# Splitting the first quad's k load by key blocks, and a new order, in a fused attention and feed-forward kernel

## The chip, the cores and the metric

One Trainium2 chip, one of its cores. The metric is the device time of one execution in microseconds (us). A core has TensorE (PE in the profile; PEld are its weight loads), VectorE (DVE), ScalarE (ACT), GpSimd (POOL) and SyncE (SP), each with its own instruction stream that is worked off in order, and 16 DMA engines that all the queues share. "SPq" and "POOLq" are DMA issues of SP and POOL.

## The reference

```python
batch, n_heads, seq, head_dim = 8, 12, 448, 64          # q, k, v: float32
scores = matmul(q, k.transpose(0, 1, 3, 2)) / sqrt(64)
attn = maximum(scores, 0.0) ** 2 / 448
x = matmul(attn, v)                                      # then [B, S, H*D] -> [3584, 768]
h = x @ w_in                                             # [768, 2048]
g = h * (1 / (1 + exp(-1.702 * h)))
out = g @ w_out                                          # [2048, 768], float32
```

## The kernel before

**Units of work.** A batch has 12 heads; four heads make a quad, so there are 24 quads, u = 0 to 23. A quad's q, k or v lies in a tile of 128 partitions x 2 x 448: a partition stands for one of two heads and one of 64 runs of 7 tokens, the middle axis for the other pair of heads, and the 448 columns are those 7 tokens of 64 numbers each. Block j is the j-th token of every run. Matmuls run in float16.

**Attention of one quad.** k and q come as float32 by a load on SP's queue (`load`, L97) and are cast on an engine (`cast`, L107), or, for quads 1 to 5, are cast on the way by a load on POOL's queue (`load_cast`, L102), which v always is. They are turned around: quads 0 to 5 by 14 transposes on TensorE against an identity (`trans_pe`, L126) and a copy out of PSUM (`trans_evac`, L136), later ones by a DMA transpose on SP's queue. `scores` (L143) makes four 64 x 64 x 448 matmuls for one block j of keys, into two PSUM banks; `relu` (L156, on ACT or DVE) copies each bank out, `square` squares both halves, `attn_v` (L173) sums over the seven blocks, and `xt_evac` copies the result to x.

**Feed-forward.** Tokens go in eight groups g of 6 or 8 blocks of 64. Group 0's first layer is 16 column parts f of six full matmuls (`m1`, in three steps); the other groups take a seven-product scheme on sums of blocks (`unit_product`), so do all groups in the second layer (`pair_product`, `single`). A gelu on ACT writes a float32 buffer (`gf`, five of them), a widening on POOL or DVE turns it into the float16 tile that the second layer reads.

**The order.** No scheduler decides it at run time: a string of some 1950 words is worked off from left to right, and each word emits one step on its engine, so every engine's stream is in the order of the words. A word is a letter for the step, its indices, `:` and an engine where that differs from the usual one, `@` and the PSUM banks (0 to 7) that it takes. `s4.0@5.4` is the scores of quad 4, block 0, in banks 5 and 4; `r4.2.1` the relu of quad 4, block 2, bank 1 of its two; `x` a square; `a3` the attention product of quad 3; `tk`, `ek` the transposes and the copy out of k (`tq`, `eq` of q); `f0.6.1` a step of the first layer; `g` a gelu, `v` a widening (usual engine POOL); `Lk`, `Lq` loads on SP; `jk`, `jq`, `V`, `jwa`, `jwb`, `jo` loads of k, q, v, w_in (two halves of each of four blocks) and w_out on POOL; `K`, `Q` casts; `G3` a small transfer on SP that waits for w_in's block 3 and so holds back the loads behind it; `I` the identity, on POOL; `z13` thirteen matmuls on zeros that write a bank nobody reads.

**The loads on POOL's queue** are 28 before the first widening stands in that stream: the float16 k, q, v of the first quads, w_in, and last the four of w_out. They use eight semaphores in turn, so the n-th load waits for the landing of the one eight before it. A transfer into a reused buffer also waits for that buffer's last reader.

**The opening of the string before**, up to the first scores, is

```python
"jq1 jk1 V0 z13@0 Lk0 K0:d z1 I tk0@1 Lq0 Q0:d jk3 ek0:a tq0@2 tq1@3 jq3 eq0 eq1 "
"s0.1@4.5 r0.1.1 r0.1.0:d s0.4@6.7 r0.4.1:d jq2 s0.6@0.1 r0.6.0:d r0.4.0 V1 r0.6.1 "
```

and around the attention product of quad 3

```python
"f0.6.0@3 f0.6.1 r4.3.0 r4.2.0:d r4.1.1 f0.6.2 g0.6 tk5@7 tq5@0 x3.6 r4.3.1:d eq5:a "
"x4.2 s4.0@5.4 v0.6 s4.4@1.2 ek5 r4.0.1 a3@3.6 r4.0.0:d S2.1 S0.3 v0.2 s4.5@0.7 "
```

Of the kernel before, what the change touches and what calls it, by code (L numbers as in the profile page):

```python
# [8 lines left out]
F32 = mybir.dt.float32  # L9
# [6 lines left out]
def kernel(  # L16
# [43 lines left out]
    def new(tag, shape, dt, name=None):  # L60
        return pools[tag].tile(shape, dt, name=name or tag, tag=tag)
# [35 lines left out]
    def load(n, u):  # L97
        x = new(f"{n}st", [128, 2, S], F32)
        nc.sync.dma_start(out=x, in_=quad(n, u))
        units[u][n + "st"] = x  # L100
# [25 lines left out]
    def trans_pe(n, p, u):  # L126
        ps = bank(p, "tr", F16)
        x = units[u].pop(n + "16")
        for j in range(J):
            for a in range(2):  # L130
                nc.tensor.matmul(  # L131
                    out=ps[64 * a:64 * a + 64, j * 128:(j + 1) * 128],
                    lhsT=x[:, a, 64 * j:64 * j + 64], rhs=ident[:, :], is_transpose=True)
        units[u][n + "ps"] = ps

    def trans_evac(n, e, u):  # L136
        t = new(f"{n}T", [128, J, 128], F16)
        copy(e, t, units[u].pop(n + "ps")[:, 0:J * 128].rearrange("p (j c) -> p j c", j=J))
        units[u][n + "T"] = t
# [283 lines left out]
    with tc.manual_schedule():  # L423
# [8 lines left out]
        for n in "kq":  # L432
            two["L" + n] = lambda e, p, u, n=n: load(n, u)
            two["j" + n] = lambda e, p, u, n=n: load_cast(n, u)
            two[n.upper()] = lambda e, p, u, n=n: cast(n, e, u)
            two["R" + n] = lambda e, p, u, n=n: trans_dma(n, u)
            two["t" + n] = lambda e, p, u, n=n: trans_pe(n, p, u)
            two["e" + n] = lambda e, p, u, n=n: trans_evac(n, e, u)
# [20 lines left out]
        def zeros(e, p, n):  # L459
# [8 lines left out]
            "jq1 jk1 V0 z13@0 Lk0 K0:d z1 I tk0@1 Lq0 Q0:d jk3 ek0:a tq0@2 tq1@3 jq3 eq0 eq1 "  # L468
            "s0.1@4.5 r0.1.1 r0.1.0:d s0.4@6.7 r0.4.1:d jq2 s0.6@0.1 r0.6.0:d r0.4.0 V1 r0.6.1 "
            "s0.3@2.3 r0.3.1:d tk1@5 ek1:a s0.0@4.7 r0.0.0 x0.1 s1.4@0.6 r1.4.0:d r0.3.0 r1.4.1 "  # L470
            "s0.2@1.3 r0.0.1 r0.2.0:d s0.5@5.4 r0.5.1:d r0.2.1 r0.5.0 s1.1@0.2 jk2 x0.3 x0.2 "
            "s1.0@6.7 r1.0.1 x0.0 tk3@1 r1.1.1 r1.1.0 jwa0 jwb0 x0.5 x1.4 r1.0.0 s1.5@4.3 x0.4 jwb2 "
            "tq3@5 jq4 r1.5.1 s1.2@7.2 s1.6@0.6 r1.5.0 x1.0 x0.6:a eq3 jk4 V2 jwa2 a0@3.4 r1.6.1:d "
            "tk2@5 ek3 r1.6.0 ek2 x1.1:a tq2@6 eq2 r1.2.1 r1.2.0 e0.0.1:a s1.3@1.0 x1.2 x1.6 jwa1 "
            "r1.3.1 jwb1 s2.3@5.6 s2.1@2.7 e0.1.1:a r1.3.0 x1.3 x1.5 r2.3.0 jk5 jq5 r2.1.1:d e0.0.0 "
            "s2.2@0.4 r2.3.1 r2.2.0 r2.2.1 a1@1.5 s3.0@7.6 x2.3:a e1.0.0:a r2.1.0:d V3 s2.0@0.4 "
            "e1.1.0 r2.0.0 e0.1.0 s2.6@2.1 jwb3 r3.0.0:d r3.0.1 s2.4@0.3 r2.6.0:d f0.3.0@7 f0.2.0@6 "
            "r2.6.1 r2.4.1:d r2.0.1 r2.4.0:d s3.2@2.1 s2.5@3.4 e1.0.1:a x2.2 f0.2.1 r3.2.1 r2.5.1 "
            "x2.1 r3.2.0 r2.5.0:d f0.3.1 x2.0:a x2.6:a s3.3@0.1 tq4@4 tk4@2 e1.1.1 V4 x2.4 r3.3.1 "
            "x2.5 jwa3 eq4 r3.3.0 a2@3.5 e2.0.1:a e2.0.0 S0.1 s3.1@1.4 ek4:a x3.3 V5 e2.1.0 jo0.0 "  # L480
            "jo1.0 f0.1.0@0 f0.1.1 f0.2.2 f0.1.2 S0.2 r3.1.1 r3.1.0 x3.1 e2.1.1:a f0.3.2 g0.1 x3.2 "
            "g0.2 f0.0.0@2 f0.0.1 x3.0 f0.0.2 g0.0 f0.8.0@3 g0.3 s3.4@4.1 r3.4.1 s3.5@5.0 r3.5.1 "
            "r3.5.0:d s3.6@6.2 r3.6.1 r3.4.0:d f0.8.1 v0.0:d x3.5 x3.4 f0.8.2 jo1.1 r3.6.0 f0.4.0@7 "
            "f0.4.1 f0.4.2 s4.2@1.0 jo0.1 G3 g0.8 v0.3 g0.4 r4.2.1 s4.1@5.2 r4.1.0 v0.4 s4.3@4.6 "
            "f0.6.0@3 f0.6.1 r4.3.0 r4.2.0:d r4.1.1 f0.6.2 g0.6 tk5@7 tq5@0 x3.6 r4.3.1:d eq5:a "
            "x4.2 s4.0@5.4 v0.6 s4.4@1.2 ek5 r4.0.1 a3@3.6 r4.0.0:d S2.1 S0.3 v0.2 s4.5@0.7 "
            "s5.0@4.5 r4.4.0 e3.0.0 e3.0.1:a f0.5.0@1 f0.5.1 f0.5.2 r5.0.0:d f0.10.0@3 x4.0 f0.10.1 "
            "r4.4.1 x4.4 r5.0.1 r4.5.1 r4.5.0 x4.5 f0.10.2 g0.5 g0.10 v0.10 s5.1@6.4 r5.1.0:d "
            "x4.1:a v0.5 r5.1.1 s4.6@2.5 s5.2@7.0 r5.2.1 r5.2.0 r4.6.1:d f0.9.0@1 x4.3 f0.7.0@3 "
            "f0.7.1 f0.7.2 f0.11.0@6 f0.11.1 f0.11.2 g0.7 r4.6.0:d x4.6:a f0.9.1 f0.9.2 S0.4 g0.11 "  # L490
            "s5.4@4.0 Lk6 g0.9 x5.1 s5.5@7.5 r5.4.1:d a4@3.2 r5.5.0 r5.4.0:d s5.6@6.1 r5.6.1 v0.7 "
            "s5.3@0.7 Lq6 r5.3.0 f0.12.0@4 x5.2 S1.1 S3.1 v0.9:d r5.3.1 r5.6.0 x5.3 f0.12.1 x5.0 "
            "f0.15.0@1 e4.0.0:a f0.14.0@0 f0.15.1 f0.15.2 r5.5.1 S2.2 x5.4 x5.5 f0.13.0@7 f0.13.1 "
            "x5.6:a u1.0.0@6 a5@3.5 Q6:a v0.8 v0.11 T1.1 f0.12.2 e4.0.1:a v0.1:d g0.15 t1.0.0 K6 "
            "S1.2 e5.0.1 u1.1.0@2 t1.1.0 u1.3.0@1 e5.0.0 u1.1.1@5 T1.2 u1.0.2 S2.3 t1.0.2 S1.4 "
            "f0.13.2 u1.0.1@3 T1.3 v0.15 g0.13 u1.0.4 f0.14.1 t1.0.4 S3.2 S1.3 v0.13 b1.0.1 T1.4 "
            "W0.1 u1.1.2 u1.0.3 Lk7 Lq8 u1.2.0@7 g1.0.1 v1.0.1 t1.1.2 u1.1.4 b1.1.1 g1.1.1 W2.1 "
            "u1.1.3 t1.1.4 u1.0.5 S3.3 b1.0.3 u1.0.6 b1.1.3 W1.1 u1.1.6 v1.1.1 g1.0.5 u1.2.1@6 W3.1 "
            "v1.0.5 b1.0.6 u1.3.1@3 g1.1.3 v1.1.3 g1.0.3 t1.2.0 b1.1.6 u1.2.2 W2.2 f0.14.2 g1.1.6 "
            "v1.1.6 W3.3 b1.2.1 g1.0.6 v1.0.6:d S3.4 p0.0.0@5 v1.0.3:d t1.3.0 u1.3.2 g0.12 K7 "  # L500
            "t1.2.2 W0.3 S2.4 g0.14 Q8:a u1.2.3 v0.14 u1.2.4 t1.2.4 W0.2 b1.3.1 v0.12:d Rk6 u1.1.5 "
            "g1.2.1 W1.2 A0.0.1@0 b1.2.3 g1.3.1 u1.3.3 W3.2 u1.2.5 p0.0.1@4 g1.1.5 v1.2.1 A0.0.2@1 "
            "g1.2.5 Rq6 h0.0.0 v1.2.5 l0.0.1 s6.0@0.2 g1.2.3 r6.0.1 r6.0.0 V6 u1.2.6 W0.4 t1.3.2 "
            "s6.1@7.2 r6.1.1 p0.0.2 A0.0.3 r6.1.0 W2.4 V8 x6.0:a h0.0.2 u1.3.4 b1.2.6 s6.5@0.2 "
            "r6.5.0 r6.5.1 Lk8 v1.1.5:d s6.2@7.6 r6.2.0 W2.3 p0.0.3 r6.2.1:d W1.3 v1.2.3 x6.5 Lq7 "
            "s6.3@0.2 t1.3.4 K8:p W3.4 r6.3.0 Rk7 b1.3.3 s6.4@7.6 p0.0.4 x6.2:a W1.4 A0.0.4 r6.4.0 "
            "h0.0.4 u1.3.5 r6.4.1 u1.3.6 l0.0.3 g1.3.5 b1.3.6 Q7 x6.4 r6.3.1 p0.0.5 l0.0.5 Rq7 "
            "s7.2@0.7 r7.2.1:d x6.3:a r7.2.0 s6.6@6.1 r6.6.1 r6.6.0:d s7.0@3.2 r7.0.0 x6.1 x6.6 Rq8 "
            "p0.0.6 r7.0.1 s7.1@5.7 g1.3.6 v1.3.6 l0.0.6 s7.4@0.1 r7.4.1 Rk8 a6@6.3 r7.4.0:d Lk9 "
            "x7.2 s7.3@2.4 s7.5@1.0 r7.1.0 x7.0:a V7 p1.0.0@5 r7.1.1:d K9:p Lq9 r7.5.0 r7.5.1:d "  # L510
            "e6.0.0 x7.4 s7.6@7.1 e6.1.1:a r7.3.0 o0.1 e6.0.1:a s8.2@0.2 r8.2.0:d g1.3.3 i0.2.0@3 "
            "r7.6.1:d e6.1.0 v1.3.1:d v1.3.5 r7.3.1 Q9 Lk11 x7.5:a r7.6.0:d x7.1 Rq9 x7.3:a "
            "s8.1@0.1 r8.2.1 n0.2.0:a s8.0@6.4 r8.1.1 Lq10 Q10 x7.6 r8.1.0 r8.0.0 A0.2.5@0 a7@7.2 "
            "e7.1.0:a r8.0.1:d e7.0.1:a e7.0.0 s8.3@3.1 r8.3.1 A1.0.1@1 r8.3.0 s8.6@0.6 r8.6.0 "
            "K11:d i0.2.1@4 h1.0.0:d s8.4@7.1 r8.6.1:d x8.2:a x8.1:a A1.0.2@0 s8.5@3.0 r8.5.0:d "
            "x8.6:a p1.0.1@6 r8.4.1 e7.1.1:a x8.0 p1.0.2 V13 r8.4.0 r8.5.1 Rk9 s9.3@3.1 n0.2.1:a "
            "s9.0@2.7 x8.3 x8.4 x8.5:a r9.3.1:d r9.0.1 l1.0.1 a8@0.4 r9.0.0:d s9.1@1.7 r9.1.1:d "
            "T2.1 g1.2.6 p1.0.3 e8.1.0:a v1.3.3 e8.0.0:a e8.1.1 Lk10 K10:p u2.1.0@2 r9.3.0 e8.0.1:a "
            "T2.2 T2.4 r9.1.0 t2.1.0 Lq11 s9.4@7.0 r9.4.1:d s9.2@3.4 r9.2.0 v1.2.6:d u2.1.1@1 "
            "b2.1.1 u2.1.2 u2.0.0@0 T2.3 t2.0.0:d u2.0.1@3 r9.4.0 Rq10 r9.2.1 Q11:a Rk10 t2.1.2:d "  # L520
            "b2.0.1 g2.1.1 v2.1.1 g2.0.1 A1.0.3 A1.2.1@1 v2.0.1 u2.2.0@7 u2.2.1@4 t2.2.0 u2.1.4 "
            "t2.1.4 b2.2.1 u2.0.2 u2.1.3 b2.1.3 u2.0.3 u2.2.2 t2.0.2 g2.2.1 g2.1.3 u2.0.4 u2.2.3 "
            "Lk12 u2.1.6 x9.3 t2.0.4 u2.0.5 Rk11 v2.2.1 K12 b2.0.3 b2.1.6 h1.0.2 v2.1.3 Lq12 t2.2.2 "
# [147 lines left out]
```

## Time and profile before

| | |
|---|---|
| median of 3 runs | 363.47 us (363.39, 363.47, 364.65) |
| the profiled execution | 364.18 us |
| its span (first to last recorded work) | 362.4 us |
| POOL, busy | 111.8 us (31%) |
| loads of k, q on POOL's queue, median to landing | 8.4 and 6.9 us |
| loads of v, of a half block of w_in, of a w_out part on it | 5.5, 12.7 and 19.9 us |
| loads of k, q on SP's queue | 4.5 and 4.3 us |
| memory read, written | 45.61 MB, 11.01 MB |

The profile is one execution; times inside it count from the start of its span. In a line of the timeline stand start, duration, engine, source line, operation, output and input tiles, the number of instructions merged into it, and in brackets how long the engine idled before and what ended that. In the view by stretches, each engine's busy time stands with the number of its instructions, then the granted TensorE clock, the share of the DMA engines in use (over 1 where queues overlap) and GB/s. The chain that ended last is followed backward from the last instruction, at each step to what released it. Where one merged line covers many matmuls its time is that of the stream, not of one.

### The profile page before, as it was taken

The page shows a single profiled execution, that of the slowest core. Times are in us where ns is not written, and L with a number is a line of the kernel's source. Part 1 is how long each engine was busy: PE and PEld are TensorE (multiplying, and loading weights), DVE is VectorE, ACT ScalarE, POOL GpSimd, SP SyncE. Part 2 cuts the span into 40 slices and gives each one's busy share as a digit, 9 for nine tenths or more (in the row PEclk, how much of TensorE's full clock was granted, in tenths as well). Part 3 has the DMA queues.
Part 4 walks back from the last instruction along what each step waited for, and adds up shares of the span by engine and source line. Part 5 has one row for each costly group of instructions (what it writes and reads, how often), then busy time and mean ns, then how long its engine had stood idle before and what let it go on. Part 6 is the DMA issues. An engine that isn't in the chain of part 4 may idle for free.

```text
span 362.4 us, 9114 instructions
## 1 busy us (share of the span) xinstructions
PE 352.5 (97%) x3598; PEld 236.0 (65%) x3598; DVE 309.1 (85%) x585; ACT 284.9 (79%) x560; POOL 111.8 (31%) x165
## 2 busy tenths in 40 slices
PE   8789999999999999999999999999999999999995
PEld 4445558855579555886569855786559855678662
DVE  3999999999997999888999799868999789875643
ACT  3999996999989997779996899878897697445420
POOL 5744522354225440155014440165021311001200
PEclk9999999999999999999999999999999999999999
DMA  8999999479999989535893764874590233003124
GB/s 182 173 200 201 215 231 228 107 149 220 196 209 189 241 158 260 165 110 79 203 213 77 216 81 118 147 152 104 115 171 4 47 110 89 2 0 89 44 67 110
DMA packets 65228, 51.39 MB, mean 142 GB/s; under 512 B 35744, under 2 KB 61856, under 8 KB 65184
## 3 DMA queue, kind: packets, MB, share of 16 engines
q1 hardware_dynamic: 48256, 36.32, 42.2%
q0 software_dynamic: 16608, 14.09, 27.0%
q8 instruction: 28, 0.46, 0.6%
q10 hardware_dynamic: 320, 0.39, 0.4%
q14 instruction: 16, 0.13, 0.1%
HBM read 45.61 MB, written 11.01 MB: 156 GB/s over the span
## 4 chain that ended last, share of the span: by engine, by line
PE 90%; DMA 5%; DVE 2%; POOL 1%; issue 0%; ACT 0%
PE hx L203 32%; PE ox L203 31%; PE sc L150 9%; PE av L181 8%; PE os L203 6%; DMA q<-in_q_dram 3%; PE ht L228 3%; DMA k<-in_k_dram 2%; PE zp L463 1%; PE tr L131 1%; DVE at L88 1%; POOL wout L415 0%; DVE at L161 0%; POOL q L104 0%; POOL v L104 0%
## 5 line engine op out<-in xcount | busy, mean ns | idle before, releaser
L163 ACT ACTIVATE at<-sc 128x448 f16<-128x448 f32 x218 | 108.2, 567 | 10.7 <-PE sc L150 9.9
L161 DVE TENSOR_SCALAR at<-sc 128x448 f16<-128x448 f32 x118 | 69.5, 614 | 3.6 <-PE sc L150 3.2
L203 PEld LDWEIGHTS <-win 128*128 128x128 f16 x672 | 61.5, 98 | 8.4 <-issue 1.8
L88 DVE TENSOR_TENSOR at<-at 128x896 f16<-128x896 f16 x109 | 65.9, 633 | 0.9 <-ACT at L163 0.2
L217 POOL TENSOR_SCALAR go<-gf 128x512 f16<-128x512 f32 x42 | 28.2, 671 | 109.9 <-ACT gf L214 108.3
L88 DVE TENSOR_TENSOR gf<-hx,gf 128x512 f32<-128x512 f32 (+1 forms) x84 | 51.6, 627 | 11.0 <-ACT gf L79 7.9
L214 ACT ACTIVATE gf<-gf 128x512 f32<-128x512 f32 (+1 forms) x84 | 47.5, 587 | 13.2 <-DVE gf L88 11.8
L169 ACT ACTIVATE at<-at 128x896 f16<-128x896 f16 x59 | 56.5, 974 | 1.1 <-DVE at L161 0.8
L217 POOL TENSOR_SCALAR ge<-gf 128x384 f16<-128x384 f32 x52 | 29.3, 563 | 73.3 <-ACT gf L214 60.8
L150 PE MATMUL sc<-qT,kT 64*64 64x448 f16 x672 | 48.9, 358 | 2.6 <-DVE qT L83 0.9
L203 PEld LDWEIGHTS <-winS 128*128 128x128 f16 x504 | 46.1, 98 | 5.5 <-issue 0.9
L79 ACT ACTIVATE gf<-hx 128x512 f32<-128x512 f32 (+1 forms) x63 | 34.5, 554 | 18.5 <-PE hx L203 15.0
L203 PE MATMUL ox<-wout,go 128*128 128x384 f16 x256 | 46.3, 326 | 0.0
L203 PEld LDWEIGHTS <-go 128*128 128x128 f16 x320 | 30.1, 98 | 22.0 <-issue 4.3
L203 PE MATMUL hx<-T,winS 128*128 128x256 f16 (+1 forms) x336 | 39.9, 261 | 0.0
L181 PE MATMUL av<-at,v 64*64 64x448 f16 x672 | 36.8, 350 | 0.9 <-ACT gf L214 0.6
L203 PEld LDWEIGHTS <-ge 128*128 128x128 f16 x256 | 24.0, 98 | 18.4 <-issue 4.5
L203 PE MATMUL hx<-xo,win 128*128 128x256 f16 x288 | 35.9, 273 | 0.0
L203 PE MATMUL ox<-wT,asum 128*128 128x384 f16 x192 | 34.9, 327 | 0.0
L150 PEld LDWEIGHTS <-kT 64*64 64x64 f16 x672 | 17.6, 105 | 24.7 <-issue 18.0
L203 PEld LDWEIGHTS <-asum 128*128 128x128 f16 x224 | 21.0, 98 | 15.7 <-issue 2.8
L181 PEld LDWEIGHTS <-v 64*64 64x64 f16 x672 | 20.3, 107 | 13.4 <-issue 2.9
(77 smaller groups left out, 452.2 us busy)
## 6 DMA issues: line engine op xcount, KB each, us to landing
out_dram<-osb SPq DMA_DIRECT2D x52, 192.0 KB, 3.9
kst<-in_k_dram SPq DMA_DIRECT2D x19, 448.0 KB, 4.5
qst<-in_q_dram SPq DMA_DIRECT2D x19, 448.0 KB, 4.3
v<-in_v_dram POOLq DMA_DIRECT2D x24, 224.0 KB, 5.5
win<-in_moe_w_in_dram POOLq DMA_DIRECT2D x8, 384.0 KB, 12.7
wout<-in_moe_w_out_dram POOLq DMA_DIRECT2D x4, 768.0 KB, 19.9
q<-in_q_dram POOLq DMA_DIRECT2D x5, 224.0 KB, 6.9
k<-in_k_dram POOLq DMA_DIRECT2D x5, 224.0 KB, 8.4
```

The source lines that it names most:

```text
L79: nc.scalar.activation(out=o, in_=i, func=AF.Copy)
L88: eng[e].tensor_tensor(out=o, in0=x, in1=y, op=op)
L131: nc.tensor.matmul(out=ps[64 * a:64 * a + 64, j * 128:(j + 1) * 128], lhsT=x[:, a, 64 * j:64 * j + 64], rhs=ident[:, :], is_transpose=True)
L150: nc.tensor.matmul(out=sc[a][c, 0:S], lhsT=st["kT"][r, j, c], rhs=st["qT"][r, :, c], start=True, stop=True)
L161: nc.vector.tensor_scalar(out=o, in0=i, scalar1=0.0, scalar2=None, op0=ALU.max)
L163: nc.scalar.activation(out=o, in_=i, func=AF.Relu)
L169: nc.scalar.activation(out=at, in_=at, func=AF.Square)
L181: nc.tensor.matmul(out=av[s][64 * a:64 * a + 64, 0:S], lhsT=v16[r, a, 64 * j:64 * j + 64], rhs=at[r, a, :], start=(j == 0), stop=(j == J - 1))
L203: nc.tensor.matmul(out=o, lhsT=lhs(i), rhs=rhs(i), start=start and i == 0, stop=i == n - 1, skip_group_check=True)
L214: nc.scalar.activation(out=o, in_=i, func=AF.Gelu_apprx_sigmoid, scale=1.0 / SC)
L217: eng[e].tensor_scalar(out=o, in0=i, scalar1=SC, scalar2=1.0, op0=ALU.mult, op1=ALU.mult)
L228: nc.tensor.matmul(out=hp[g, f][:, 0:n], lhsT=w[:, i, fo:fo + 128], rhs=xts[g][:, i, 0:n], start=i == 0, stop=i == NK - 1)
```

## The change

The load, the cast, the transposes and the copy out can now each do one part of a tile, by an index h: part 0 is key blocks 0 to 3 (256 columns), part 1 blocks 4 to 6 (192 columns). Only k of quad 0 uses it. Its two loads stand behind the load of q on SP's queue; before, the whole k stood ahead of q. The zero products go from 14 in one row to 9, then two single ones behind the transposes of k's first part. The whole string of words is another one: the same steps apart from these, in another order, with other banks, and some relus, squares, copies and casts on other engines.

```diff
+    KH = (slice(0, 256), slice(256, S))
+
+    def load(n, u, h=None):
+        st = units[u]
+        if not h:
+            st[n + "st"] = new(f"{n}st", [128, 2, S], F32)
+        c = slice(0, S) if h is None else KH[h]
+        nc.sync.dma_start(out=st[n + "st"][:, :, c], in_=quad(n, u)[:, :, c])
...
+    def cast(n, e, u, h=None):
+        if h is not None:
+            if h == 0:
+                units[u][n + "16"] = new(f"{n}16", [128, 2, S], F16)
+            x = units[u][n + "st"] if h == 0 else units[u].pop(n + "st")
+            copy(e, units[u][n + "16"][:, :, KH[h]], x[:, :, KH[h]])
+            return
...
+    def trans_pe(n, p, u, h=None):
         ps = bank(p, "tr", F16)
-        x = units[u].pop(n + "16")
-        for j in range(J):
+        x = units[u][n + "16"] if h == 0 else units[u].pop(n + "16")
+        for j in range(J) if h is None else range(4 * h, 4 + 3 * h):
...
+        j = slice(0, J) if h is None else slice(4 * h, 4 + 3 * h)
+        copy(e, st[n + "T"][:, j, :],
+             st.pop(n + "ps")[:, 0:J * 128].rearrange("p (j c) -> p j c", j=J)[:, j, :])
...
-            "jq1 jk1 V0 z13@0 Lk0 K0:d z1 I tk0@1 Lq0 Q0:d jk3 ek0:a tq0@2 tq1@3 jq3 eq0 eq1 "
-            "s0.1@4.5 r0.1.1 r0.1.0:d s0.4@6.7 r0.4.1:d jq2 s0.6@0.1 r0.6.0:d r0.4.0 V1 r0.6.1 "
...
+            "Lq0 Q0:d jk1 I z9@0 tq0@1 eq0:a jq1 Lk0.0 K0.0:d tk0.0@2 V0 ek0.0 z1 z1 s0.0@3.4 "
+            "r0.0.1 Lk0.1 K0.1:d s0.3@5.6 r0.3.1:d r0.0.0 x0.0 tk1@7 r0.3.0 s0.1@1.2 r0.1.0 "
+            "r0.1.1:d jq2 tk0.1@0 s0.2@4.6 ek0.1:a s0.6@3.5 jk3 x0.3 r0.2.1 jk2 tq1@1 r0.2.0 "
...
+            "f0.8.2 s4.3@1.7 r3.5.1 g0.1 x3.5 s4.2@3.5 g0.8 v0.8 r3.4.0 x3.3:a s4.1@2.0 r4.1.1 "
+            "r4.3.1 f0.6.0@4 f0.6.1 f0.6.2 g0.6 f0.4.0@6 S2.1 r4.1.0:d r4.3.0:d f0.4.1 f0.4.2 g0.4 "
+            "v0.4 tk5@0 r4.2.0:d tq5@7 r4.2.1 x4.3 s4.4@4.2 s4.0@1.6 x3.4:a a3@3.5 ek5 eq5 r4.0.1 "
...
```

The loads on POOL's queue go, before, in the order jq1 jk1 V0 jk3 jq3 jq2 V1 jk2 jwa0 jwb0 jwb2 jq4 jk4 V2 jwa2 jwa1 jwb1 jk5 jq5 V3 jwb3 V4 jwa3 V5 and the four of w_out; now jk1 jq1 V0 jq2 jk3 jk2 jq3 jwb0 V1 jwa0 V2 jq4 jk4 jwb2 jwa1 jwa2 jwb1 jq5 jk5 V3 jwa3 jwb3 V5 V4 and the four of w_out.

## The prediction

> **What bounds the kernel now.** I read the page's busy shares first, then the busy time by stretches of time, then the timeline of the opening, then the chain that ended last around the point where TensorE's idling stops.
>
> ```profile
> span 362.4 us, 9114 instructions
> ...
> PE 352.5 (97%) x3598; PEld 236.0 (65%) x3598; DVE 309.1 (85%) x585; ACT 284.9 (79%) x560; POOL 111.8 (31%) x165
> ```
>
> TensorE (PE) is busy for 352.5 of 362.4 us, so 9.9 us is all that any order of the work could take from its idle time. The stretches say where those 9.9 us are.
>
> ```profile
> core 0: us, PE busy (x) PEld busy (x) DVE busy (x) ACT busy (x) POOL busy (x), PEclk, DMA share, GB/s
> 0.00:9.06 9.06, 7.49 (x72) 4.48 (x73) 3.25 (x8) 2.98 (x5) 5.11 (x12) 1.00 0.85 182
> 9.06:18.10 9.04, 7.07 (x106) 3.73 (x105) 9.04 (x18) 9.04 (x19) 6.38 (x10) 1.00 1.17 173
> 18.10:40.00 21.90, 19.82 (x278) 11.36 (x282) 20.85 (x44) 20.66 (x46) 11.53 (x16) 1.00 1.30 200
> 40.00:80.00 40.00, 40.00 (x385) 27.03 (x377) 38.55 (x74) 36.10 (x71) 15.04 (x22) 1.00 0.99 186
> ...
> 340.00:362.40 22.40, 18.12 (x116) 11.02 (x113) 11.39 (x20) 4.65 (x9) 2.17 (x3) 0.99 0.34 90
> ```
>
> From 40 us on TensorE has no idle time at all until its last matmul at 358.1; the 4.3 us after that are the last add and the stores. The idle time is in the first 40 us: 1.57, 1.97 and 2.08 us in the three first stretches. There VectorE (DVE) and ScalarE (ACT) are full from 9 us on and the DMA engines are full too (share over 1). So the end is the moment at which TensorE passes its last wait, plus a sum of matmuls that does not depend on how it got there. That last wait is at 39.30, where a3, the attention product of quad 3, starts:
>
> ```profile
> 24.64 11.21 DMA q<-in_q_dram
> 36.13 0.87 POOL wout L415
> 37.27 0.88 POOL wout L415
> 38.22 0.52 POOL ge L217
> 38.76 0.50 ACT gf L214
> 39.30 1.52 PE av L181 x28
> ```
>
> Read upward: a3 needs a PSUM bank that the gelu g0.6 empties; that gelu is the seventh, there are five gf buffers, DVE's widening v0.0 has freed one for the sixth, and the first widening on GpSimd (POOL) frees the next at 38.74; that widening stands in POOL's queue behind the four issues of w_out, and these wait for earlier loads to land. The last of the four is issued at 37.27 after the load of v for quad 3 (issued 25.34, 11.6 us to landing: 36.94). ACT sits idle 0.82 us before g0.6, TensorE 0.61 us before a3. This is the gate for all that follows.
>
> **The change part by part.** Counted from the two word lists, every matmul of the two kernels is the same but for three zero products; there is one more load issue on SP, one more cast and one more copy out of PSUM. All other differences are order.
>
> *The opening.* These rows price it:
>
> ```profile
> 1.15 4.66 PE L463 MATMUL zp<-wT 128*128 128x384 f16 x14 [1.15 <-DVE wT L456]
> 4.29 0.63 DVE L83 CAST k<-kst 128x896 f16<-128x896 f32 x1 [3.19 <-DMA kst<-in_k_dram]
> 5.48 0.63 DVE L83 CAST q<-qst 128x896 f16<-128x896 f32 x1 [0.56 <-DMA qst<-in_q_dram]
> 5.75 0.96 PE L131 MATMUL tr<-ident,k 128*64 128x128 f16 x14
> 6.75 0.92 ACT L79 ACTIVATE kT<-tr 128x896 f16<-128x896 f16 x1 [4.52 <-PE tr L131]
> 8.02 0.95 PE L150 MATMUL sc<-qT,kT 64*64 64x448 f16 x16 [0.33 <-DVE qT L83]
> 8.45 2.22 DVE L161 TENSOR_SCALAR at<-sc 128x448 f16<-128x448 f32 x4
> ```
>
> Now q goes first on SP's queue and takes k's landing: 4.24, cast until 4.92. Its 14 transposes (0.96) run 4.95 to 5.91, the copy by ACT (0.92) ends at 6.87. The first 256 of 448 columns of k land between q's 4.24 and 5.46, when all of the second load had landed; in proportion 4.24 + 1.22 x 256/448 = 4.94. Cast 0.63 x 4/7 = 0.36 to 5.30 (5.82 at worst), 8 transposes behind q's, 8/14 of 0.96 = 0.55, to 6.46, copy by DVE 4/7 of its 0.58 = 0.33, to 6.8. Then come two zeros of 4.66/14 = 0.333 each, 6.46 to 7.12. So the first score is at about 7.1 instead of 8.02: 0.9 earlier, with bounds 0 (the extra SP issue of 0.45 and the cast push k back to where it was) and 1.15 (zeros free, ACT's copy decides at 6.87). The first relu moves with it, 8.45 to 7.5. The second part of k (cast 0.27, six transposes 0.41, copy 3/7 of 0.92 = 0.39) lies beside the relus of the first blocks. The three zeros that go (3 x 0.333 = 1.0) lie in time in which TensorE waits for q anyway: nothing.
>
> *Rule against it.* 333 ns a zero of 384 columns, against 8 products of 384 columns in 1.30 us (163 ns) later: at the start TensorE runs at half its later pace, though the granted clock reads 1.00, and the first 14 transposes take 0.96 against 0.58 for later ones. The Trainium skill (TensorE: Matmul & The Clock Gate, part 1) says the array runs at half rate until about 3.4 us of sustained activity, and that idling returns it there. Nine zeros end at 1.15 + 3.0 = 4.15, and TensorE then idles until 4.95. By the rule the first scores may run at half pace, some 0.2 us later each; by the rows of before they would not. Either is smaller than the slack found below.
>
> *The load of k for quad 2.* Before, it is the eighth load on POOL's queue, lands at 18.34 and TensorE, DVE and ACT idle 0.86, 0.80 and 0.41 us around it. Now it is sixth; the sixth load of before (q of quad 2, issued 8.4) landed at 15.3, and it is wanted at about 17. That wait goes: worth 0 to 0.8, I take 0.5, since DVE and ACT, not TensorE, set the pace there.
>
> So ACT, DVE and TensorE come to the gate 0.9 + 0.5 = 1.4 us earlier (0 to 2.0), with the same work done: up to it both kernels have 31 scores, 21 first-layer parts, 43 relus on ACT; what moves between ACT and DVE nearly cancels (ACT: one copy and one square more, 0.3 + 1.0, and 0.92 x 3 less 0.92 + 0.39 of k/q copies saved).
>
> *The gate itself.* The new order has the same gate: the sixth gelu, g0.6, takes the buffer that DVE's v0.3 frees, the seventh, g0.4, waits for POOL's first widening, v0.8, and that stands behind the same four w_out issues, the last of them again waiting for v of quad 3, again the 20th load of POOL's queue with the same 19 ahead of it, in another order. The DMA engines are full between (about 200 GB/s), so it lands when those bytes are through. What can move it is the start of that queue: 144 GB/s between 7 and 9 us, when little more than v of quad 0 and a load issued at 7.01 was in flight. Now a load is issued at about 5.95, when q's transposes are done. At 200 instead of 144 these 2 us carry 112 KB more, 0.56 us. Against that, the next loads are issued 0.3 to 0.6 later than before (they wait for transposes of k in two steps). I take 0.5 earlier, bounds 1.2 earlier (the low rates up to 13 us filled as well) and 0.8 later.
>
> *Behind the gate.* Before, a3 followed g0.6 at once. Now g0.4 is followed on ACT by the relu r4.2.1 (0.47), which frees one of a3's two banks, and the square x3.4 (0.97), which a3's fifth block needs: a3 starts 0.5 later and loses some 0.25 inside. Less two switches between half-array and full matmuls that no longer lie behind this point, 0.11 each (ox of 8: 1.41 after scores, 1.30 otherwise). Together +0.5.
>
> *After it.* Before lost nothing there, so a new order can only lose: I add 0.1, bounds 0 and 1.0; The queues that the order moves have cover there. On SP the gate on w_in block 3 now waits for the 22nd load of POOL's queue, not the 21st, so k and q of quad 6 behind it go out some 2 us after the 39.85 and 40.45 of before; their casts by ACT began at 52.5, so 8 us cover it, and beyond that quad 6's first score (73.0) would be late. On POOL v of quad 4 falls from 22nd to 24th place, landing near 42.9 where it was 40.6; a4 starts near 47.3. The w_out parts change places; their first sum by DVE was at 59.5. The end (last product, add, stores) has the same steps.
>
> Sum against the profiled execution, span 362.4: -0.5 + 0.5 + 0.1 = +0.1; the 1.4 us saved in the opening is spent waiting at the gate. The profiled execution took 364.18, 1.8 more than its span and 0.7 above the median of the runs, 363.47 (363.39 to 364.65). Since before and after are read against that median, and the bounds lean to the fast side, I set 363.3.
>
> **The rivals.** (1) The gate opens with the opening: the loads run ahead by 1.2 or more, and the order behind g0.4 costs nothing, so 1.2 to 2.0 of the earlier start reaches the end: 361.5 to 362.3. For it: 7 to 13 us shows 144, 169, 124 GB/s, room to fill. Against: POOL issued the loads that landed in 9 to 18 us four or more us ahead, so issue was not their limit. (2) Slower: POOL's queue falls behind. Loads five to seven wait for transposes in TensorE's own order; if they come 0.8 late and nothing refills it, v of quad 3 lands at 37.7, and with the 0.5 behind the gate and a later stall of up to 1.0 the time is 364.5 to 365.8. It decides from the point where that landing is later than 36.94. For it: the issue times; against: the queue of eight loads is full from 13 us on. (3) The change does not do what it says: k's first part lands with the second, the first score stays at 8.0. The gate hides this: 363.5, the forecast's time.
>
> **How the numbers follow.** Forecast, gate holds (rival 3 within it): 0.56, own range 362.7 to 364.1. Rival 1: 0.27. Rival 2: 0.17. A difference of 0.5% (1.8 us) is about what a measurement of this kernel can tell from no change. Faster by more (under 361.65) is about two thirds of rival 1, 0.18; slower by more (over 365.3) needs most of rival 2's terms at once, 0.10; the rest 0.72. The range takes in both rivals but for their far ends: 361.5 to 365.0.
>
> **What would show it.** First score near 7.1; the idle before the transposes of quad 2's k gone; POOL's first widening again near 38; ACT idle 1.5 to 2.5 us before g0.4; a3 within 0.5 of 39.3; no idle of TensorE later. It is wrong if a3 starts before 38.3 or after 40.3, or if TensorE idles behind it.

## The result, and the profile after

The changed kernel takes 369.21 us (median of 4 runs, 368.82 to 369.55) where the kernel before takes 363.59 beside it: ratio 1.0148, 95% interval 1.0125 to 1.0171. It is slower, by 5.6 us; the forecast was no change (363.3). The profiled execution took 369.55, its span is 5.3 us longer than before. The page's first lines, the changed kernel:

```profile
span 367.7 us, 9122 instructions
...
PE 354.4 (96%) x3595; PEld 236.3 (64%) x3595; DVE 311.7 (85%) x578; ACT 285.4 (78%) x566; POOL 113.9 (31%) x168
```

Busy times hardly move, so the loss is waiting and stretched work. Its busy times by stretches:

```profile
core 0: us, PE busy (x) PEld busy (x) DVE busy (x) ACT busy (x) POOL busy (x), PEclk, DMA share, GB/s
0.00:9.06 9.06, 7.02 (x59) 3.48 (x59) 2.89 (x8) 3.65 (x6) 3.70 (x10) 1.00 0.90 190
9.06:18.10 9.04, 7.25 (x128) 4.20 (x130) 8.68 (x17) 8.69 (x19) 6.98 (x10) 1.00 0.98 137
18.10:40.00 21.90, 19.58 (x259) 10.24 (x254) 20.35 (x41) 19.47 (x44) 10.84 (x15) 1.00 1.25 203
40.00:80.00 40.00, 39.60 (x381) 27.13 (x381) 38.47 (x74) 36.99 (x72) 14.97 (x22) 1.00 0.98 187
80.00:120.00 40.00, 39.41 (x420) 26.53 (x420) 36.56 (x66) 35.97 (x76) 15.70 (x21) 1.00 1.09 216
...
160.00:200.00 40.00, 38.60 (x391) 25.08 (x390) 35.93 (x66) 31.71 (x63) 12.68 (x18) 1.00 0.56 132
```

Two things are new. From 9 to 18 us the DMA engines carry 137 GB/s where they carried 173. And TensorE idles behind the gate, which it never did before: 0.4, 0.6 and 1.4 us in these stretches. The chain that ended last, around the gate:

```profile
25.08 12.81 DMA v<-in_v_dram
...
38.18 0.87 POOL wout L428
39.05 0.08 issue
39.13 0.52 POOL ge L230
39.65 0.02 issue
39.67 0.50 ACT gf L227
...
40.59 1.43 PE av L194 x21
```

It is the gate of before, step by step, but for its first link. Before, the chain ran through q of quad 5, landed at 35.84, and the last two issues of w_out, with v of quad 3 landing at 36.94, just as the first of the two ended. Now v of quad 3 alone sets it: it lands at 37.89, and everything behind it is 0.9 later.

To find where the rest went, take the start of each attention product a_n and add what TensorE still has to do from there, counted from the words at the steady durations of its rows (0.19 for four scores, 1.32 for an attention product, 1.30 for a pair product and so on). In a stretch without loss this projected end stays put; where it grows, time was lost. All numbers are us, each from one profiled execution; the columns e1 to e13 are experiments below. The last row is the span less the row above it.

| | before | after | e1 | e2 | e6 | e7 | e13 |
|---|---|---|---|---|---|---|---|
| a4 | 358.0 | 359.2 | 359.8 | 357.5 | 358.1 | 357.7 | 359.1 |
| a8 | 358.1 | 359.7 | 359.8 | 357.8 | 358.7 | 358.2 | 359.6 |
| a9 | 358.2 | 360.7 | 360.0 | 358.8 | 358.7 | 359.3 | 359.7 |
| a12 | 358.1 | 360.7 | 359.9 | 358.7 | 358.7 | 359.3 | 359.8 |
| a14 | 358.1 | 361.9 | 359.9 | 359.9 | 359.9 | 360.4 | 359.9 |
| a15 | 358.0 | 363.0 | 359.9 | 361.0 | 360.6 | 360.4 | 360.1 |
| a23 | 358.1 | 363.0 | 360.1 | 361.0 | 360.7 | 360.4 | 360.1 |
| tail | 4.3 | 4.8 | 4.2 | 4.8 | 4.7 | 4.7 | 4.1 |

So of the 5.3 us 1.2 are lost up to a4 (the gate), 0.5 between a4 and a8, 1.0 between a8 and a9, 2.3 between a12 and a15, and 0.5 in the tail (together a little more than 5.3, as the projected end drifts by 0.1 in the old order too).

### The profile page after: what moved, and what is told of

It is laid out like the page before. It is cut to its first block, busy times and chain, and to the rows that moved or that the text cites. A ratio compares the mean times of both kernels' runs of the same rounds, so it can differ in the third digit from the quotient of the medians.

```text
span 367.7 us, 9122 instructions
## 1 busy us (share of the span) xinstructions
PE 354.4 (96%) x3595; PEld 236.3 (64%) x3595; DVE 311.7 (85%) x578; ACT 285.4 (78%) x566; POOL 113.9 (31%) x168
## 4 chain that ended last, share of the span: by engine, by line
PE 78%; DVE 6%; ACT 6%; DMA 4%; issue 3%; POOL 1%; DVEq 0%; POOLq 0%; ACTq 0%
PE hx L216 28%; PE ox L216 27%; PE sc L163 8%; PE av L194 7%; PE os L216 5%; DMA v<-in_v_dram 3%; ACT at L176 3%; PE ht L241 2%; DVE gf L88 1%; DMA qst<-in_q_dram 1%; DVE at L88 1%; DVE at L174 1%; ACT at L182 1%; ACT gf L227 1%; PE tr L141 1%
## 5 line engine op out<-in xcount | busy, mean ns | idle before, releaser
L176 ACT ACTIVATE at<-sc 128x448 f16<-128x448 f32 x226 | 111.1, 568 | 9.0 <-PE sc L163 8.1
L174 DVE TENSOR_SCALAR at<-sc 128x448 f16<-128x448 f32 x110 | 65.3, 618 | 5.9 <-PE sc L163 4.5
L227 ACT ACTIVATE gf<-gf 128x512 f32<-128x512 f32 (+1 forms) x84 | 48.5, 588 | 20.9 <-DVE gf L88 20.8
L230 POOL TENSOR_SCALAR go<-gf 128x512 f16<-128x512 f32 x47 | 32.0, 680 | 101.9 <-ACT gf L227 100.8
L182 ACT ACTIVATE at<-at 128x896 f16<-128x896 f16 x63 | 60.2, 976 | 0.6 <-DVE at L174 0.3
L163 PE MATMUL sc<-qT,kT 64*64 64x448 f16 x672 | 51.8, 362 | 3.0 <-DVE at L174 0.6
L230 POOL TENSOR_SCALAR ge<-gf 128x384 f16<-128x384 f32 x48 | 26.2, 545 | 58.4 <-ACT gf L227 56.8
L216 PE MATMUL hx<-xo,win 128*128 128x256 f16 x288 | 36.7, 273 | 0.0
L163 PEld LDWEIGHTS <-kT 64*64 64x64 f16 x672 | 18.7, 105 | 27.0 <-issue 20.0
```

What stands on the lines that cost most here:

```text
L163: nc.tensor.matmul(out=sc[a][c, 0:S], lhsT=st["kT"][r, j, c], rhs=st["qT"][r, :, c], start=True, stop=True)
L174: nc.vector.tensor_scalar(out=o, in0=i, scalar1=0.0, scalar2=None, op0=ALU.max)
L176: nc.scalar.activation(out=o, in_=i, func=AF.Relu)
L182: nc.scalar.activation(out=at, in_=at, func=AF.Square)
L216: nc.tensor.matmul(out=o, lhsT=lhs(i), rhs=rhs(i), start=start and i == 0, stop=i == n - 1, skip_group_check=True)
L227: nc.scalar.activation(out=o, in_=i, func=AF.Gelu_apprx_sigmoid, scale=1.0 / SC)
```

## The experiments

Each was timed beside the kernel before, and its ratio is to that. Words are moved in the string; nothing else changes unless the diff says so. Each profile is one execution, and executions of one of these kernels differ by 2 to 5 us, so a profile shows where time went in that execution, and only the times show what a kernel usually takes.

### Opening and late order apart: e1, e2, e3

```diff
-(new words 1 to 1957)
+e1: (new words 1 to 230) (what is left, in the old order)
+e2: (old words 1 to 227) (what is left, in the new order)
+e3: (new words 1 to 94) (what is left, in the old order, one bank renamed)
```

> The first 230 words of the new order (all up to about 43 us: the split k, the opening, the loads, the opening of the gate at a3 and what goes with it), then what is left of the old order, no bank renamed. The words behind the cut are the old ones, so this keeps the new opening and throws away the new late order. Theory L (most of the loss lies in the new late order itself): the new opening costs what it cost at the gate, 0.7 to 1.2, and the tail is the old one: 364.1 to 365.2, ratio 1.002 to 1.005. Theory K (the late gate works on: every later stretch starts behind its loads or casts and loses there too): 367.5 or more, ratio over 1.010.

> The mirror of it: the first 227 words of the old order (one load and one cast of k, gate as before at 39.3), then what is left of the new order. Theory L: it loses all that the new order lost behind the gate and in the tail, about 4: 367.0 to 368.6, ratio 1.010 to 1.014. Theory K: with the gate as before nothing is lost later: 363.4 to 364.4, ratio under 1.003. Both parts equal would give 365.5 to 366.5 here and in its mirror.

> Only the first 94 words of the new order (up to the first x evictions at about 24 us), then what is left of the old order (one bank renamed). The POOL queue ran dry at 9 to 11 us in the new kernel, and these words are kept; the v loads and the w_out loads behind them have the old order again. If the dry queue alone makes the gate late, the last w_out load, and a3, are late by 0.5 to 1.0 here too: 364.0 to 365.0. If the gate is late because of the order of the loads between 24 and 36 us (v of quad 3 put far ahead, w_out behind it), the gate is as before: 363.2 to 363.9.

Measured: e1 365.47, ratio 1.005 (1.0026 to 1.0073); e2 367.42, 1.0101 (1.0067 to 1.0134); e3 366.25, 1.0065 (1.0039 to 1.009). Theory L holds, e1 a little above its times: the halves add to what the whole change lost. The columns of e1 and e2 show the same: e1 loses at the gate and is flat behind it; e2 has an early gate (a3 at 38.92) and every later loss (a8 to a9 1.0, a12 to a15 2.3, tail 0.5). So the late loss is no echo of the late gate. In e3 a3 came at 41.16 (39.30 before, 40.22 after), and its time is above both expectations, so the first 24 us suffice to make the gate late. How much of that is the load queue is open: in the profile of e3 the granted clock read 0.50 from 22.3 to 26.0 us, in that of e1 (a3 at 40.92) from 15.0 to 18.8, and in those of the two kernels nowhere.

### The split alone: e4

```diff
-jq1 jk1 V0 z13@0 Lk0 K0:d z1 I tk0@1 Lq0 Q0:d jk3 ek0:a tq0@2 tq1@3 jq3 eq0
+Lq0 Q0:d jq1 I Lk0.0 Lk0.1 z13@0 z1 jk1 V0 tq0@1 eq0:a K0.0:d tk0.0@2 ek0.0
+K0.1:d tk0.1@0 ek0.1:a jk3 tq1@3 jq3
```

> The old order with one edit: q's load and cast first, k of quad 0 loaded, cast, transposed and evicted in two parts behind it, 14 zero matmuls as before, and all words from the second q on as they were. If the split as such moves the first score to about 7.2 to 7.6 and the loads stay in step, the gate sets the time: 363.0 to 363.8. If the half pace of TensorE after the opening is set by the zeros alone, the transposes here run at full pace from 6.5 on, and the gate is not late. Rival: the half pace lasts until about 9 us here too, jk3 and what is behind it on POOL are late by 0.5 to 1, and the kernel ends at 364 to 365.

Measured: 365.66, ratio 1.0046 (1.0023 to 1.007), above both expectations; the profiled span is 362.8, a3 at 39.84, in one of the faster executions (364.6). The loads are late as the rival says, but not for its reason: from 6.3 on TensorE was at full pace (8 transposes in 0.39). k of quad 3 is issued at 8.15 (7.01 before), since it takes the k16 slot of quad 0's k, and that is free only when the second part is transposed. The first score did not come earlier (8.16 against 8.02).

### A free slot for quad 0's k: e5 (in the changed kernel), e8 (in the kernel before)

```diff
-units[u][n + "16"] = new(f"{n}16", [128, 2, S], F16)
+units[u][n + "16"] = new("at", [128, 2, S], F16)
```

In e8 the same tile is taken where the whole k of quad 0 is cast.

> The changed kernel with one edit: the 16-bit tile of quad 0's split k is taken from the pool of attention tiles, which is nearly empty then, and not from the two k16 tiles. So k of quad 3 does not wait for a transpose: its slot is free, and POOL can issue it at about 6.5 (behind q of quad 2) where it was 9.33. Theory S (the late gate comes from the two k16 slots, which the split holds for longer): the gap of the DMA queues at 9 to 10 us closes, a3 moves from 40.2 to 39.0 to 39.5, and the time falls by 0.7 to 1.2: 368.0 to 368.5, ratio 1.012. Theory C (the half pace of TensorE after 9 zeros makes it late): the scores and transposes up to 9.3 are as slow as before, a3 stays at 40.0 to 40.5, 369. Rival: the early load takes DMA time from k's second part, which lands later, and the first squares with it: no gain or a loss of up to 0.5.

> The kernel before, with the same edit as the changed one above: quad 0's k in a tile of the attention pool, so that k of quad 3 waits for no transpose (it was issued at 7.0, behind a wait of 2.8 for quad 0's transposes). If the two k16 slots hold up the gate in the old kernel too, a3 goes from 39.3 to 38.3 to 39.0 and the time to 362.5 to 363.3, ratio 0.997 to 0.999. If what follows on POOL (its eight issues in flight, the bytes until the last w_out load) sets the gate, it stays within 0.3: 363.2 to 363.8. Rival: the earlier load delays q and k of quad 0, and the first scores come after 8.02.

Measured: e5 368.25, ratio 1.0133 (1.0107 to 1.0159), a3 at 38.88; e8 363.21, 0.9985 (0.9964 to 1.0007), a3 at 37.76. In e8 k of quad 3 goes out at 4.14 and a3 comes 1.5 earlier than before, so in the old order the slots do hold up the gate; the time is not told apart from that of the kernel before, and lies where its two expectations meet. In e5 it does not tell S from C: TensorE was at full pace from 5.0 on in that execution, and e6 and e7, which have the two slots and the same pace, had a3 at 39.12 and 38.63.

### The pace at the start: e9 (the changed kernel again), e10

```diff
-e9: z9@0
+e10: z14@0
```

> The changed kernel once more, unedited. In its first profile TensorE worked at half pace until 9.3 (14 transposes in 0.96) and a3 came at 40.2; the edited kernels that share its opening showed half pace until 9.1 in one profile and full pace from 5.0 on in three, with a3 between 38.6 and 41.2. If the pace after 9 zeros differs from execution to execution, this profile has a3 either near 38.6 to 39.2 (full pace at 5.0) or at 40.0 or later (half pace), the first score at 6.6 or 7.1, and the times spread by more than 1.5. The late stretches do not depend on it: a8 to a9 loses 1.0, a12 to a15 2.3, as in the first profile. Time 368.8 to 369.6; with full pace in most executions 367.0 to 368.5.

> The changed kernel with 14 zero matmuls at the start where it has 9 (the two later ones stay). Theory C (the fewer zeros leave TensorE at half pace until 9 us in some executions, and through k of quad 1 and POOL's queue that makes the gate late): with 14 the pace is full from about 6.3 in every execution, as in the kernels that have 14; the first transposes start 0.8 later (5.8), the first score at 7.3 to 7.6, k of quad 3 is issued at 8.3 to 8.8, a3 at 39.0 to 39.8 with a small spread; time 0.3 to 1.0 below that of the changed kernel on this chip if half pace is common there, 0.3 above if it is rare. Rival: the zeros make no difference to the pace, and the later start of the transposes moves everything, a3 included, 0.8 later.

Measured: e9 370.41, ratio 1.018 (1.0133 to 1.0227); e10 369.15, 1.0162 (1.0106 to 1.0219), so the two are not told apart; e9 is above its expectation. The timelines show what differs from execution to execution. The changed kernel in its first profile:

```profile
7.17 0.96 PE L163 MATMUL sc<-qT,kT 64*64 64x448 f16 x8
8.06 0.96 PE L141 MATMUL tr<-ident,k 128*64 128x128 f16 x14
9.33 1.52 POOL L108 DMA_DIRECT2D k<-in_k_dram  x2 [2.24 <-PE tr L141]
```

The same kernel in e9:

```profile
6.58 0.57 PE L163 MATMUL sc<-qT,kT 64*64 64x448 f16 x8 [0.24 <-ACT qT L79]
7.08 0.58 PE L141 MATMUL tr<-ident,k 128*64 128x128 f16 x14
7.97 1.43 POOL L108 DMA_DIRECT2D k<-in_k_dram  x2 [1.38 <-DVE at L174]
```

Half pace in one, full pace in the other, and POOL's next load 1.4 earlier: k of quad 3 takes the slot of quad 1's k, the second row of the two views. Of ten profiles with 9 zeros, four were at half pace until about 9 us (after, e3, e11, e13); all seven with 14 zeros were at full pace from 5.5 to 6.5. That fits the zeros setting the pace, but so few profiles, most of the second group in the old order, don't show it. And e9 had a3 at 40.01 for all its pace, and e10, where theory C had 39.0 to 39.8, at 41.48 (in an execution of 372.94, far above its median): more is in the gate than that.

What goes with it is the DMA engines' load. From 10 to 11 us, in the kernel before and in the changed one:

```profile
10.00:11.00 1.00, 0.27 (x10) 0.17 (x10) 1.00 (x3) 1.00 (x3) 1.00 (x2) 1.00 1.15 174
10.00:11.00 1.00, 0.58 (x12) 0.24 (x10) 1.00 (x3) 1.00 (x4) 0.75 (x2) 1.00 0.42 25
```

The stretches 10 to 18 us of four kernels, before, after, e12 and e15 in this order (from 6 to 10 us they carried 164, 188, 204 and 204 GB/s):

```profile
10.00:14.00 4.00, 2.89 (x52) 1.57 (x52) 4.00 (x9) 4.00 (x10) 2.69 (x4) 1.00 1.08 150
14.00:18.00 4.00, 3.25 (x45) 1.56 (x40) 4.00 (x8) 4.00 (x9) 2.83 (x4) 1.00 1.27 197
```

```profile
10.00:14.00 4.00, 3.06 (x53) 1.54 (x50) 3.81 (x8) 4.00 (x10) 2.99 (x6) 1.00 0.89 120
14.00:18.00 4.00, 3.16 (x65) 2.23 (x62) 4.00 (x9) 4.00 (x10) 3.31 (x5) 1.00 1.12 158
```

```profile
10.00:14.00 4.00, 3.49 (x56) 1.85 (x57) 4.00 (x9) 4.00 (x11) 2.16 (x5) 1.00 1.23 191
14.00:18.00 4.00, 3.75 (x64) 2.20 (x63) 4.00 (x8) 4.00 (x9) 3.75 (x6) 1.00 1.20 190
```

```profile
10.00:14.00 4.00, 4.00 (x54) 2.31 (x54) 2.80 (x6) 2.19 (x5) 1.44 (x3) 0.50 0.49 68
14.00:18.00 4.00, 3.51 (x42) 1.71 (x38) 3.16 (x7) 4.00 (x10) 2.70 (x4) 0.50 1.19 180
```

From 22 to 38 us these four carry 198 to 207 GB/s: nothing is caught up there. So I compare what was carried from 6 to 18 us (rate by time, three stretches of four) with when a3 came. With the old order of loads: 2.34 MB and a3 at 37.46 (e12), 2.24 and 37.76 (e8), 2.11 and 38.92 (e2), 2.04 and 39.30 (before), 1.94 and 39.84 (e4), 1.81 and 41.91 (e15): at 205 GB/s 0.1 MB is 0.5 us; from e12 to e4 a3 moves 0.6 for each 0.1 MB, and e15 lies well above that line. With the new order it is looser: 2.12 to 2.14 MB and 38.6 to 39.1 (e5, e6, e7), 2.03 to 2.06 and 40.0 to 40.1 (e9, e14), 2.00 and 41.5 (e10), 1.82 to 1.86 and 40.1 to 40.5 (after, e11, e13), 1.75 and 40.9 (e1); e3, with half of each order, had 1.88 and 41.2. This is a correlation over seventeen profiles, with e8 and e12 as the runs in which the queue was filled on purpose. A second thing goes with a late a3: in e1, e3, e14 and e15 the granted clock fell to 0.50 for some 3.7 us or longer ahead of it, in e14 from 26.0 to 29.7. e14 and e5 have the same opening and were both at full pace early, and a3 came at 40.07 and 38.88 (2.03 and 2.12 MB). One stretch of e14:

```profile
27.00:28.00 1.00, 1.00 (x7) 0.40 (x4) 1.00 (x3) 0.61 (x2) 0.12 (x1) 0.50 1.23 204
```

### The late losses: e6, e7

```diff
-e6: ... V10 v2.0.1:d Q12 v2.2.3 ...    Q17        K18:p
+e6: ... V10 v2.0.1:d v2.2.3 Q12 ...    Q17:a      K18:a
-e7: ... r15.3.0 s15.5@7.0 ... Lq19 h3.0.2:d p3.0.4
+e7: ... r15.3.0 h3.0.2 s15.5@7.0 ... Lq19 p3.0.4
```

> The changed kernel with three casts moved: q of quad 12 stays on POOL but goes one widening later (from 116.3 to about 119), q of quad 17 and k of quad 18 go from POOL to ScalarE (188 to 190.5). Nothing else. Theory P (a POOL cast beside a 16-bit tensor_tensor of VectorE holds that one up: 1.82 for 0.62 at 115.9, 1.41 for 0.69 at 189.6): the square at 115.9 takes 0.6 again, the stretch a8 to a9 gives back 0.7 to 1.0 of its 1.0, the sum at 189.6 takes 0.7 and the wait of 1.10 at 192.0 falls to about 0.4: time 367.5 to 368.2, ratio 1.010 to 1.012. Theory D (VectorE has too much to do there, whoever is beside it): the durations stay long or the next wait takes their place; 368.9 to 369.5.

> The changed kernel with one word moved: the snapshot of the pair product that the wait of 1.10 at 192.0 ends on goes from VectorE, behind two sums, to ScalarE, where it stands ahead of two relus (ScalarE had 0.52 free at 188.9). The casts stay. Theory D (VectorE is the bound from 185 to 200: busy 5.00, 4.79 and 4.84 of 5.00): TensorE gains only the 0.54 that is taken off VectorE, and loses the rest again before 200: 368.6 to 368.9. Theory W (the one late snapshot is what TensorE lacked): the 1.10 is gone and stays gone: 368.0 to 368.3. If POOL's casts are all of it: 369 and the wait returns one product later.

Measured: e6 368.38, ratio 1.015 (1.0109 to 1.0191); e7 368.18, 1.0123 (1.0095 to 1.0152). The intervals do not tell them from the changed kernel; the profiles do (of executions of 367.14 and 366.86, the fastest or nearly so of their kernels). The changed kernel between a8 and a9:

```profile
115.53 0.75 POOL L108 DMA_DIRECT2D v<-in_v_dram  x1
115.89 1.82 DVE L88 TENSOR_TENSOR at<-at 128x896 f16<-128x896 f16 x1
116.28 0.94 POOL L83 CAST q<-qst 128x896 f16<-128x896 f32 x1
120.00 0.66 PE L216 MATMUL hx<-xe,win 128*128 128x192 f16 x6 [0.59 <-ACT gf L79]
```

A square that takes 0.61 elsewhere takes 1.82 and ends 0.49 after POOL's cast. In e6, with the cast one widening later:

```profile
114.80 0.61 DVE L88 TENSOR_TENSOR at<-at 128x896 f16<-128x896 f16 x1
117.10 0.93 POOL L83 CAST q<-qst 128x896 f16<-128x896 f32 x1
```

The square takes 0.61, the wait is gone, and a8 to a9 loses 0.1 instead of 1.0: theory P at that place. The issue of v's load on POOL (0.75 from 114.44) still lies beside the square in e6, so it was the cast that held it up. Around 190 us the changed kernel has

```profile
189.12 1.32 POOL L83 CAST k<-kst 128x896 f16<-128x896 f32 x1
189.57 1.41 DVE L88 TENSOR_TENSOR go<-go,asum 128x1024 f16<-128x1024 f16 x1
191.37 0.54 DVE L85 TENSOR_SCALAR osb<-ox 128x384 f32<-128x384 f32 x1
191.97 1.46 PE L216 MATMUL ox<-wout,go 128*128 128x384 f16 x8 [1.10 <-DVE osb L85]
```

where the casts are only part: e6 took them off POOL, the sum took 0.69 and the wait fell to 0.17, but the casts on ScalarE brought a new wait of 0.30, and 0.4 of 1.1 came back. In e7 the casts stayed and the snapshot (`osb<-ox`, which must read the bank before p3.0.4 adds to it) went to ScalarE: a14 to a15 loses nothing any more. Theory W, not D, by the profile.

### Repairs added up: e11, e13, e14

```diff
+e11: Q12 as in e6, h3.0.2 as in e7, the last 23 words as before
-e13: Q18:d e12.0.0 e12.1.0:a     r15.0.1:d
+e13: e12.0.0 e12.1.0:a Q18:d     r15.0.1       (and e11)
+e14: e13, and the free slot of e5
```

> The changed kernel with three repairs together: the cast of q of quad 12 one widening later on POOL (as in the run of the casts), the snapshot of the pair product on ScalarE (as in the run of the snapshot), and the last 23 words (the stores and last products of the tail) in the old order. The two first gave back 0.9 (a8 to a9) and 1.15 (a14 to a15) in their own runs. If the losses are separate, they add: 2.05, and 0.5 for the tail, so 2.5 below the changed kernel: 366.3 to 367.1, ratio 1.005 to 1.008; what is left is the gate and a12 to a14 (1.2). If the loss only moves on (VectorE stays the bound), less than 1.5 comes back: over 367.5.

> The repairs of e11 and two more words: the cast of q of quad 18 on VectorE goes behind the last eviction of attention product 12 (it stood two evictions ahead), and one relu of quad 15 goes from VectorE, where it stood behind a sum, to ScalarE, which had 1.07 free at 186.3. Theory V (VectorE's order holds up the banks of the next scores): a12 to a13 gives back 0.4 to 0.5 and a13 to a14 0.5 to 0.7, so that only the gate is left of the loss; 365.5 to 366.3 where e11 had 366.9, ratio 1.003 to 1.006. Theory D (VectorE is simply full from 175 to 195): the loss moves to the next score or product, and a12 to a15 together keep 0.8 or more.

> The same, and quad 0's k in a tile of the attention pool, as in e5 and e8. If the causes found are all of the loss, what is left against the kernel before is the gate, at 38.6 to 39.5 (before 39.3), and 0.3 to 0.5 between a3 and a6: 363.4 to 364.6, ratio 0.999 to 1.003. If something else is lost in the new order, 365 or more.

Measured: e11 366.91, ratio 1.0081 (1.005 to 1.0111); e13 367.48, 1.0098 (1.0068 to 1.0128); e14 365.52, 1.0058 (1.0032 to 1.0084); profiled spans 365.3, 364.2 and 363.6. e11 is as expected, and its interval lies below the changed kernel's, so the repairs together show in the time too. The times are above the expectations of e13 and e14, and e13's median is not better than e11's: it scatters from 365.3 to 368.7, and its profiled execution took 366.03. So what its two words gain is seen in the profile only, where they did what theory V said. The changed kernel:

```profile
175.24 1.24 PE L163 MATMUL sc<-qT,kT 64*64 64x448 f16 x12
186.13 0.56 PE L163 MATMUL sc<-qT,kT 64*64 64x448 f16 x5
186.90 0.38 PE L163 MATMUL sc<-qT,kT 64*64 64x448 f16 x3 [0.21 <-DVE at L174]
```

and e13:

```profile
174.34 0.76 PE L163 MATMUL sc<-qT,kT 64*64 64x448 f16 x12
184.75 0.57 PE L163 MATMUL sc<-qT,kT 64*64 64x448 f16 x8
```

Twelve scores take 0.76 again where they were stretched to 1.24, without any idle time to show for it, and eight run in one piece. With the snapshot that is three words, and they bring a12 to a15 from 2.3 to 0.3, although the collision at 188 us is still there (1.41 for the sum): with the snapshot elsewhere nobody waits for it. The tail is back at 4.1 with the old last words. What e13 still loses against before is the gate (1.1), 0.5 between a4 and a8 and those 0.3. e14 at 365 or more is the branch in which something else is still lost; in its profile that is the gate (a3 at 40.07).

### A version that beats both: e12, and e15 with the split

```diff
+e12: the old order, with e8's free slot and v0.3:d for v0.3
+e15: e4 (the split in the old order) with the same two edits
```

> The kernel before with two edits in its opening: k of quad 0 in a tile of the attention pool (as in the run before, where a3 came at 37.8 where it was 39.3), and the first widening on VectorE, so that the gate does not wait for POOL to issue the last w_out load. If POOL's queue is still what the gate waits for, the second edit moves a3 a further 0.5 to 1.2 earlier, to 36.6 to 37.3: 361.9 to 362.8, ratio 0.993 to 0.996. If the squares, relus or the v load of quad 3 are next in line, a3 stays at 37.5 to 37.9: 362.6 to 363.4, ratio 0.997 to 0.999.

> The split in the old order (as e4), with quad 0's k in a tile of the attention pool and the first widening on VectorE (as e12). Beside e12 only the split differs: q first, k in two parts. If the split only lost time through the slot, this is as e12 or better: first scores at 7.2 to 7.7, a3 at 37.0 to 37.6, 362.3 to 363.0, ratio 0.995 to 0.998. If the split is of no use because the loads behind it set the gate, the first scores come earlier and a3 does not: within 0.4 of e12. If it costs something of its own (two parts of 0.43 to cast and evict, the second k of quad 0 landing later), a3 is at 38 or later: 363.2 to 364.

Measured: e12 362.79, ratio 0.9966 (0.9941 to 0.999), span 360.5, a3 at 37.46: faster than both kernels, if by little. a3 is only 0.3 earlier than in e8, as expected where something other than POOL's queue is next in line. e15 363.78, 1.001 (0.9988 to 1.0031): the split seems to give e12's gain back, though the two intervals just overlap. Its profile is of its slowest execution, 366.66, so it shows what can happen and not the usual case. There k's second part takes 7.7 to land beside the early load of k for quad 3 (5.2 in e4, which has no early load) and is cast at 9.46; TensorE waits 3.51 for it, and the first scores run at 11.09 (7.38 in e12).

## Why the prediction failed, step by step

- **The opening.** Right for the first score: 7.17 against 7.1, or 6.58 at full pace; the first relu came at 7.81, 0.3 later than predicted. But nothing of the 1.4 reached the gate: ScalarE was done with what stands ahead of the seventh gelu at 38.77, before at 37.94, and idled 0.90 there where I had 1.5 to 2.5.
- **The wait for k of quad 2.** Not gone but moved: TensorE waits 0.60 for q of quad 3 at 17.9 and 1.21 for k of quad 4 at 27.1. ScalarE and VectorE are busy 8.69 and 8.68 of 9.04 us from 9 on, no longer all of it.
- **The rule on the clock.** I set both prices of it aside as "smaller than the slack found below". The scores' price was; but k of quad 1 is transposed at the same pace, and its slot in k16 is what POOL's next load waits for (9.33 at half pace, 7.97 at full). That path was in the diff of the two orders and not in my sum, where the three zeros that go stood at nothing.
- **The gate: 0.5 earlier, bounds 1.2 earlier and 0.8 later.** The first widening started 0.91 later (39.13 against 38.22), outside the bounds. The direction was wrong because I let q of quad 2, issued at 6.37 (predicted 5.95), stand for the queue. The two loads behind it came 2.3 later (9.33 against 7.01), where I had "0.3 to 0.6 later", and the DMA engines ran nearly dry at 10 us (25 GB/s). The mechanism of rival 2 is what happened: v of quad 3 at 37.89, where it had 37.7.
- **Behind the gate: +0.5.** Right in size. The wait was not ahead of a3, which followed its gelu by 0.05 as before, but inside it: 2.02 for 1.52.
- **After it: +0.1, bounds 0 and 1.0.** This step failed, and it is most of the error: 3.7 from a4 to a23 and 0.5 in the tail. I read the full TensorE of before as a property of the work and bounded a new order by how the old one behaved. The old order had no loss there because each eviction, cast and snapshot stood where its engine reached it in time. In the new one a cast two places too early, a relu behind a sum, a snapshot behind two sums and a cast on POOL beside a square cost 0.5, 0.6, 1.1 and 0.9, by their places in the profiles. All four are visible in the words, as places on VectorE's stream, had I followed the banks of each score back to the engine that empties them.
- **Rivals.** Rival 2 had the right mechanism with 364.5 to 365.8, short by the late losses. Rival 1's gain is there to be had, but not by this change: e12 opens the gate 1.8 earlier and gains 0.9 of the time.

Open: the 0.3 to 0.5 between a5 and a6, why a3 in the new order scatters from 38.6 to 41.5 at like pace (the granted clock of 0.50 on the way is part of it at most: e9 and e10 had none ahead of a3), and how often an execution starts at which pace. None of these was tried by itself.

## What to carry to other kernels

Where the DMA engines are full up to the gate, bytes not carried at the start went here with a later gate: look for what the next load's buffer waits for, not only for what the first load brings. A newly planned order has to be followed over its whole length: for each accumulator bank, ask which engine empties it and what stands ahead of that on its stream. Here VectorE's stream, 85% busy, had no room for four misplaced words, and stretched matmuls hid part of the loss from the idle times; the projected end showed it.

## What the runs showed of the hardware

**A cast on POOL stops a 16-bit square on VectorE** (1.82 for 0.61). The Trainium skill (SBUF — State Buffer, "SBUF: two separate sides") says that the two engines share a port pair that is locked for a whole instruction, by whichever starts first, so that the other blocks. The end of the square 0.49 after the cast's end agrees with the blocking, and so does the cast's 1.32 (0.94 alone) beside the sum; the order does not, as the square's record starts 0.39 ahead of the cast's.

**TensorE can fall back to half pace after a wait of 2.2 us.** e10 at the gate:

```profile
41.48 0.38 PE L163 MATMUL sc<-qT,kT 64*64 64x448 f16 x3 [2.17 <-ACT gf L227]
41.48 2.57 PE L194 MATMUL av<-at,v 64*64 64x448 f16 x28
43.79 1.01 PE L163 MATMUL sc<-qT,kT 64*64 64x448 f16 x8
44.74 2.52 PE L241 MATMUL ht<-xe,win 128*128 128x384 f16 x10
```

Ten first-layer matmuls take 2.52 where they take 1.80, and the granted clock reads 0.50 from 43 to 45 us. So the wait cost more than itself: e10's projected end grew by 2.1 between a3 and a4, where the other kernels with these words lose 0.5 or nothing in that place. In e15, in and after a wait of 3.51, the clock read 0.50 from 9 to 19 us. The length of the wait does not decide it: the clock also fell in e14 after a wait of 1.09 and in e3 during one of 1.93, and stayed at 1.00 in e9 after one of 1.79. The Trainium skill (TensorE: Matmul & The Clock Gate, "Part 1: The HAM clock gate") puts the change at a free-running window of about 3.4 us; the scatter at the start (full pace after 9 zeros in six profiles of ten) agrees with that, the waits of 1.1 to 2.2 are shorter than such a window, and the 10 us in e15 are longer.
